# Transformer block with shared keys on one core: last burst cut 384 and 128, w2 kept as tile pairs, wo split on GpSimd, new attention orders

## The chip, the cores and the metric

The kernel runs on one core of a Trainium2 chip: TensorE (PE) multiplies, VectorE (DVE), ScalarE (ACT) and GpSimd (POOL) work on elements, and SyncE (SP) issues most DMAs. Each engine takes its own instructions strictly in the order in which they were written and waits at semaphores for the others. The metric is the device time of one launch in microseconds (us). Three runs of the kernel before took 893.58 to 894.96 us, with a median of 894.08 us.

## What is computed

With x of 2048 rows and 448 columns, 16 heads of 28, one key and one value head that all heads share, and an MLP of 1792 columns:

```python
def _A_ref(x, wq, wk, wv, wo):
    q = (x @ wq).reshape(B, S, H, Dh).transpose(0, 2, 1, 3)
    k = x @ wk
    v = x @ wv
    scores = jnp.einsum("bhqd,bkd->bhqk", q, k) * (Dh ** -0.5)
    p = _softmax(scores, axis=-1)
    o = jnp.einsum("bhqk,bkd->bhqd", p, v)
    return o.transpose(0, 2, 1, 3).reshape(B, S, H * Dh) @ wo

def _B_ref(x, w1, b1, w2, b2):
    y = _layernorm(x, axis=-1)
    h = _gelu(jnp.einsum("bsd,df->bsf", y, w1) + b1)
    return jnp.einsum("bsf,fd->bsd", h, w2) + b2

xn = _layernorm(x, axis=-1)
return x + _A_ref(xn, ...) + _B_ref(xn, ...)
```

All is float32. Where a product is made of float32r operands, each operand is split into a high and a low part and three products are summed (high by high, high by low, low by high).

## The kernel before

The 2048 rows are 16 row tiles of 128, in four chunks of four (512 rows). The program has three stages: norms and the projections of q, k and v (to about 71 us); the MLP, chunk by chunk (to about 349 us); attention with the output projection (to the end).

**MLP.** Slot `n` of the loop at L635 runs `mlp1` for one of the 14 column tiles of the hidden layer (11 matmuls, then three ACT and three DVE operations and a subtraction on POOL that make the high part `hh` and the low part `hl`), and `mlp2` for the tile two slots earlier (12 matmuls: four row tiles by three terms). w2 is not ready when the stage begins: `w2_split(s)` cuts the raw rows of two column tiles, 2s and 2s+1, into a high part on ACT (L381) and a low part on DVE (L382), and issues the load of a later pair. In the first chunk (c = 0) it is called at ft = 0, 3, 5, 7, 9, 11 and 13 (L654), always behind `mlp1` of the same slot. The high parts of all 14 tiles are one tile `w2h`, the low parts one tile `w2l`.

**Attention.** A unit is 512 queries by four heads; there are 16 units, four for each chunk, and each has 16 key tiles of 128. For each key tile `scores` makes 12 matmuls (four heads side by side in the rows of the array, three terms), one PSUM bank for each head, and then ACT takes the exponentials of the four banks (L625) into a tile `p`. The 2nd argument of `scores`, the number behind an `s` in the order, says by its bits which neighbouring banks are taken by one ACT instruction: `s6` makes one of one bank and one of three (1+3), `s5` 2+2, `s2` 1+2+1, `s4` 1+1+2, `s1` 2+1+1, `s0` four of one. Banks that are not neighbours, since the ring of eight wraps round, are never joined. `pv`, a `P` with a number of key tiles behind it, multiplies the exponentials by the values (`vs`, in which a column of ones gives the sums) into one PSUM bank, and DVE adds that bank to `oc` (L733; L731 for the first of a unit).

The PSUM banks are a ring of eight: every `s` takes the next four, every `P`, `m` and `Q` the next one. Who takes a bank must wait until the one that had it eight takes earlier has been read out, by ACT for an `s` bank and by DVE for the others.

What sets the order is the table `ORDERS` (L34 to L36): one line for units 0 to 3, one for units 4 to 14, one for the last. Two key tiles are scored ahead while the MLP ends, so the `s` of a line are two key tiles ahead of its `P`. Beside `s` and `P` there are `m` (find the shift for the exponentials of the next unit: one matmul, four DVE operations, a small DMA), `Q` (output projection of one row tile of the chunk before: 12 matmuls), `T` (the part of it that can be done early for the last chunk: 9 matmuls) and `E3` (the last burst). `load_unit(u + 1)` is issued on SP when unit u starts, and `m` reads what it loads.

When the last `P` of a unit is done, `norm_jobs` puts three DVE operations behind the next `P` and three more, and a POOL subtraction, behind the third `P`.

`split_out` cuts wo into a high and a low part (two passes over 1792 columns on DVE). It is called behind the third word of unit 0. The first use of its result is the first `Q`, in unit 4.

**Last burst.** `last_burst` multiplies the last three key tiles of unit 15 in two halves of 256 queries. Each half goes through a chain of five DVE operations, and the second one also through six small ones of `flag`; then two matmuls for each half (L776) finish the four row tiles, which are added to the rest on DVE (row tile 1: ACT copies, POOL adds) and stored, by SP for row tiles 0 and 2 and by ACT's queue for 1 and 3.

Of the kernel before, what the change touches and what calls it, by code (L numbers as in the profile page):

```python
# [10 lines left out]
F32 = mybir.dt.float32  # L11
F32R = mybir.dt.float32r
# [18 lines left out]
MLP_ORDER = 1, 2, 3, 0  # L31
HD = D // 2
WEIGHTS = 7
ORDERS = ("s5 P1 s6 s6 P2 s6 s5 P2 s4 s1 m P2 s6 P1 s6 s5 P2 s6 s6 P2 s6 s5 P2 s6 s4 P2",  # L34
          "s5 P1 s6 s6 P2 s6 s5 P2 s6 s6 P2 s6 s5 P2 s2 s2 P2 s2 m Q s2 s6 P3 s6 s4 P2",
          "s5 P1 s6 s6 P2 s6 s5 P2 s6 s6 P2 s6 s5 P2 s2 s2 P2 s2 m Q s2 s6 P2 T T T E3")  # L36
FIRST_BANK = 0
LIMITS = 0.25, 2.0 ** 40

# [2 lines left out]
def block_kernel(ctx, tc, x, wq, wk, wv, wo, w1, b1, w2, b2, out):  # L42
# [4 lines left out]
    def f(t):  # L47
        return t.bitcast(F32)
# [327 lines left out]

    def w2_split(s):
        raw = wl_q.pop(0)
        ab = slice(2 * s, 2 * s + 2)

        act.activation(w2h[:, ab, :], raw, AF.Copy, scale=0.5)  # L381
        dve.scalar_tensor_tensor(w2l[:, ab, :], raw, 0.5, f(w2h[:, ab, :]), op0=ALU.mult, op1=ALU.subtract)  # L382
        if s + 2 < NF // 2:
            w2_load(s + 2)

# [189 lines left out]
    def mlp2(c, ft, then=None):  # L575
        if ft == 0:
            m2s[c] = [bank(CT + k, (P, D)) for k in range(CT)]
        m2 = m2s[c]
        hh, hl = hs.pop((c, ft))
        terms = ((hh, w2h), (hh, w2l), (hl, w2h))  # L580
        parted = c == 0 and ft == 0
        if parted:
            for k in range(CT):
                for i, (h, w) in enumerate(terms[:2]):
                    pe.matmul(m2[k], h[:, k * P:(k + 1) * P], w[:, ft, :], start=(i == 0), stop=False)
        for k in range(CT):
            for i, (h, w) in enumerate(terms):
                if parted and i < 2:
                    continue
                pe.matmul(m2[k], h[:, k * P:(k + 1) * P], w[:, ft, :], start=(ft == 0 and i == 0),  # L590
                          stop=(ft == NF - 1 and i == 2))
# [87 lines left out]
    woh, wol = weights_tile(), weights_tile()  # L679

    def split_out():
        dve.tensor_copy(woh, wor)
        dve.tensor_sub(wol, wor, f(woh))


    sums = keep.tile([P, NU, CW // 32], F32, name="sums")
# [62 lines left out]
    def last_burst(n, flag):  # L749
        u = NU - 1  # L750
        c, g = units[u]
        oc = pos.pop(u)
        tr, rb = (att.tile([P, CW], F32, name=name) for name in ("tr2", "tr"))
        rc = att.tile([P, CW // 32], F32, name="rc")
        halves = [(slice(256 * i, 256 * i + 256), slice(8 * i, 8 * i + 8)) for i in range(2)]
        sides = []
        for h, r in halves:
            po = score_bank()[:, 0:256]
            for k in range(NT - n, NT):
                for j in range(4):  # L760
                    pe.matmul(po[32 * j:32 * j + 32, :], vs[:, k, :], ps[u, k][:, j, h],
                              start=(k == NT - n), stop=(k == NT - 1))
            sides.append(po)
        ahead(CT - 1)
        for i, (h, r) in enumerate(halves):
            dve.tensor_add(oc[:, h], oc[:, h], sides[i])
# [4 lines left out]
            dve.transpose(blocks(rb[:, h]), rc[:, r, None].to_broadcast([P, 8, 32]))  # L771
            dve.tensor_mul(oc[:, h], oc[:, h], rb[:, h])
            if i == 1:
                copy()
            for k in (2 * i, 2 * i + 1):
                pe.matmul(outs[k], oc[:, k * P:(k + 1) * P], wor[:, g, :], start=False, stop=True)  # L776
        for k in range(CT):
            a = rows[c, k]
            if k == 1:
                act.activation(tr[:, 0:D], outs[k], AF.Copy)  # L780
                pool.tensor_add(a, a, tr[:, 0:D])
            else:
                dve.tensor_add(a, a, outs[k])
            (nc.scalar if k % 2 else nc.sync).dma_start(ov[:, CT * c + k, :], a)
# [117 lines left out]
```

## Time and profile before

| | us |
|---|---|
| median of three runs | 894.08 |
| the profiled execution, its own time | 893.52 |
| its span on the core | 891.7 |
| TensorE busy in the span | 875.2 (98%) |
| ScalarE busy | 650.1 (73%) |
| VectorE busy | 360.7 (40%) |
| GpSimd busy | 155.3 (17%) |

The mean granted clock of TensorE is 0.997. Times in the rows are counted from the start of the span; 1.8 us of the profiled execution lie outside it. In a timeline row stand the start, the length, engine and line, what is written and read, the shape, how many instructions were merged, and in brackets how long the engine sat idle before and what ended that. A float32 matmul of `pv` shows as two instructions, so a `P2` counts x16 and an `s` x12. Matmuls overlap, so the time that a burst holds TensorE is read from its start to the start of the next one, not from its length. Now and then a matmul's record is missing.

### The profile page before, as it was taken

Reading aid. Unit: us, or ns where it says so; the run is one execution under the profiler, and the core shown is the slowest. Engines: PE = TensorE matmul, PEld = TensorE weight load, DVE = VectorE, ACT = ScalarE, POOL = GpSimd, SP = SyncE. Lnnn points to the kernel's source line nnn. Section 1 sums busy time; section 2 is a strip of 40 time slices with the busy share of each in tenths; the row PEclk is TensorE's granted clock in tenths of the full one; section 3 lists DMA queues with packets and bytes.
Section 4 is the critical chain, followed back from the end, with each engine's and each line's share of the span. In section 5 each row is a group of like instructions: output and inputs, shape, how many; then the busy total and the mean of one; then the engine's idle time right before and its main releaser. Section 6 shows DMA issues by size and latency. Waiting matters only on the chain.

```text
span 891.7 us, 16976 instructions
## 1 busy us (share of the span) xinstructions
PE 875.2 (98%) x6997; PEld 529.5 (59%) x6997; DVE 360.7 (40%) x654; ACT 650.1 (73%) x890; POOL 155.3 (17%) x149
## 2 busy tenths in 40 slices
PE   9999999999999999899999999999999999999997
PEld 8877888888888886333434444444444444444444
DVE  7865454335345353342343234233233233333323
ACT  5765443333443436799999898898898899899891
POOL 7443243242234332000000000000000000000000
PEclk9999999999999999999999999999999999999999
DMA  9792112002001103000002101102101102102001
GB/s 301 215 288 81 42 63 83 1 1 83 21 21 51 44 11 91 9 22 22 9 16 64 33 1 33 33 2 74 32 1 33 33 1 74 33 1 73 12 1 54
DMA packets 28957, 46.02 MB, mean 52 GB/s; under 512 B 4542, under 2 KB 20492, under 8 KB 28876
## 3 DMA queue, kind: packets, MB, share of 16 engines
q1 hardware_dynamic: 27468, 44.32, 16.1%
q8 instruction: 56, 0.92, 0.4%
q10 hardware_dynamic: 1408, 0.57, 0.2%
q14 instruction: 25, 0.20, 0.1%
HBM read 28.22 MB, written 14.68 MB: 48 GB/s over the span
## 4 chain that ended last, share of the span: by engine, by line
PE 87%; ACT 7%; issue 2%; DVE 2%; DMA 1%; SPq 0%; DVEq 0%; ACTq 0%
PE banks L618 24%; PE banks L739 23%; PE banks L180 15%; PE banks L590 15%; ACT p L625 5%; PE banks L701 4%; PE banks L185 2%; PE banks L183 2%; PE banks L304 1%; PE banks L523 1%; DMA xl<-in_A_wo_dram 1%; DMA qd<-qe 0%; DVE w2l L382 0%; PE banks L776 0%; DMA rows<-in_A_x_dram 0%
## 5 line engine op out<-in xcount | busy, mean ns | idle before, releaser
L625 ACT ACTIVATE p<-banks 128x1024 f32<-128x1024 f32 (+2 forms) x623 | 484.8, 879 | 39.5 <-PE banks L618 36.4
L618 PE MATMUL banks<-xh,ks 32*128 32x512 f32 x3072 | 256.1, 424 | 6.4 <-DVE oc L733 4.3
L618 PEld LDWEIGHTS banks<-xh,ks 32*128 32x128 f32 x3072 | 145.0, 183 | 168.0 <-ACT p L625 142.7
L739 PE MATMUL banks<-p,vs 128*32 128x512 f32 x2008 | 243.4, 601 | 0.0
L733 DVE TENSOR_TENSOR oc<-oc,banks 128x512 f32<-128x512 f32 x115 | 78.9, 686 | 304.0 <-PE banks L739 245.9
L739 PEld LDWEIGHTS banks<-p,vs 128*32 128x32 f32 x2008 | 52.2, 109 | 120.9 <-issue 80.4
L564 ACT ACTIVATE hx<-banks,b1t 128x512 f32<-128x512 f32 x56 | 38.5, 688 | 110.7 <-PE banks L185 103.7
L572 POOL TENSOR_TENSOR hl<-hx,hh 128x512 fp32r<-128x512 f32 x56 | 76.8, 1371 | 182.3 <-DVE hh L571 176.9
L723 POOL TENSOR_TENSOR otl<-oc,oth 128x512 fp32r<-128x512 f32 x15 | 19.2, 1280 | 487.7 <-DVE oth L722 487.7
L566 DVE SCALAR_TENSOR_TENSOR hz<-hz,hx 128x512 f32<-128x512 f32 x56 | 44.3, 792 | 101.6 <-ACT hz L565 101.3
L590 PE MATMUL banks<-w2l,hh 128*128 128x448 f32 x220 | 81.0, 368 | 0.8 <-DVE w2l L382 0.7
L590 PE MATMUL banks<-w2h,hl 128*128 128x448 f32 x224 | 81.4, 366 | 0.0
L590 PE MATMUL banks<-w2h,hh 128*128 128x448 f32 x220 | 81.0, 368 | 0.1
L567 ACT ACTIVATE hz<-hz 128x512 f32<-128x512 f32 x56 | 35.4, 632 | 48.5 <-DVE hz L566 48.5
L180 PE MATMUL banks<-xl,w1h 128*128 128x512 f32 x168 | 65.7, 391 | 0.0
L180 PE MATMUL banks<-xh,w1l 128*128 128x512 f32 x168 | 65.6, 391 | 0.0
L180 PE MATMUL banks<-xh,w1h 128*128 128x512 f32 x168 | 65.5, 390 | 0.0
L568 DVE SCALAR_TENSOR_TENSOR hx<-hz,hx 128x512 f32<-128x512 f32 x56 | 39.1, 698 | 42.9 <-ACT hz L567 42.9
L590 PEld LDWEIGHTS banks<-w2l,hh 128*128 128x128 f32 x220 | 41.3, 188 | 7.1 <-DVE w2l L382 3.2
L590 PEld LDWEIGHTS banks<-w2h,hh 128*128 128x128 f32 x220 | 41.3, 188 | 6.0 <-issue 0.7
L590 PEld LDWEIGHTS banks<-w2h,hl 128*128 128x128 f32 x224 | 42.1, 188 | 3.3
L565 ACT ACTIVATE hz<-banks,b1s 128x512 f32<-128x512 f32 x56 | 38.2, 682 | 0.0
(156 smaller groups left out, 765.3 us busy)
## 6 DMA issues: line engine op xcount, KB each, us to landing
xh<-qd SPq DMA_DIRECT2D x64, 112.0 KB
qd<-qe SPq DMA_DIRECT2D x12, 512.0 KB
a<-in_A_x_dram SPq DMA_DIRECT2D x24, 224.0 KB
ad<-a SPq DMA_DIRECT2D x16, 224.0 KB
row<-ad SPq DMA_DIRECT2D x16, 224.0 KB
raw<-in_B_w_dram SPq DMA_DIRECT2D x7, 448.0 KB
out_dram<-row SPq DMA_DIRECT2D x14, 224.0 KB
ks<-qe SPq DMA_DIRECT2D x16, 112.0 KB
```

The source lines that it names most:

```text
L180: pe.matmul(ps, w, v, start=(n == 0), stop=False)
L564: act.activation(hx, ph, AF.Identity, bias=b1t[:, ft:ft + 1])
L565: act.activation(hz, ph, AF.Square, bias=b1s[:, ft:ft + 1], scale=GELU[0] ** 0.5)
L566: dve.scalar_tensor_tensor(hz, hz, 1.0, hx, op0=ALU.add, op1=ALU.mult)
L568: dve.scalar_tensor_tensor(hx, hz, 1.0, hx, op0=ALU.add, op1=ALU.mult)
L572: pool.tensor_sub(hl, hx, f(hh))
L590: pe.matmul(m2[k], h[:, k * P:(k + 1) * P], w[:, ft, :], start=(ft == 0 and i == 0), stop=(ft == NF - 1 and i == 2))
L618: pe.matmul(bank(at[j]), ks[rs, i, keys], qss[u][rs, h, :], start=(n == 0), stop=(n == 2))
L625: act.activation(p[:, j:j + n, :], banks[:, at[j]:at[j] + n, :], AF.Exp, scale=SCALE)
L701: pe.matmul(po, ots[c, g][o][:, ts], w[:, g, :], start=(n == 1), stop=(stop and n == 3 * len(gs)))
L733: dve.tensor_add(pos[u], pos[u], po)
L739: pe.matmul(po[32 * j:32 * j + 32, :], vs[:, k, :], ps[u, k][:, j, :], start=(k == kt), stop=(k == kt + n - 1))
```

## The change

Five things are changed.

1. `ORDERS` is new. Units 0 to 3 now have `P1` behind every `s`. Units 4 to 14 have `s P1` eight times, then `s6 P2 s4 s4 m Q s0 s1 P3 s6 s4 P2 s2 P1`; the last unit begins in the same way and ends in `s6 T T T E3`. The ACT instructions of the exponentials go from 629 (332 of one bank, 199 of two, 98 of three) to 802 (598, 186 and 18).
2. `split_out` runs on POOL and is called behind the third word of unit 2.
3. w2's parts are 14 tiles, a high and a low one for each pair, and `w2_split` is called in the even slots 0, 2, ..., 12.
4. The last burst is cut into 384 and 128 queries, so three row tiles hang on the first part and one on the second.
5. At the end row tiles 0 and 1 go through ACT and POOL (in before row tile 1 only), with a tile `half` of their own, and 2 and 3 through DVE.

```diff
-ORDERS = ("s5 P1 s6 s6 P2 s6 s5 P2 s4 s1 m P2 s6 P1 s6 s5 P2 s6 s6 P2 s6 s5 P2 s6 s4 P2",
-          "s5 P1 s6 s6 P2 s6 s5 P2 s6 s6 P2 s6 s5 P2 s2 s2 P2 s2 m Q s2 s6 P3 s6 s4 P2",
...
+ORDERS = ("s2 P1 s4 P1 s2 P1 s2 P1 s1 P1 m s2 P1 s4 P1 s2 P1 s2 P1 s2 P1 s4 P1 s4 P1 s4 P1 s2 P1 s2 P1 s2 P1",
+          "s2 P1 s2 P1 s2 P1 s2 P1 s2 P1 s4 P1 s4 P1 s0 P1 s6 P2 s4 s4 m Q s0 s1 P3 s6 s4 P2 s2 P1",
...
     def w2_split(s):
         raw = wl_q.pop(0)
-        ab = slice(2 * s, 2 * s + 2)
-
-        act.activation(w2h[:, ab, :], raw, AF.Copy, scale=0.5)
-        dve.scalar_tensor_tensor(w2l[:, ab, :], raw, 0.5, f(w2h[:, ab, :]), op0=ALU.mult, op1=ALU.subtract)
+        high, low = w2s[s]
+        act.activation(high, raw, AF.Copy, scale=0.5)
+        dve.scalar_tensor_tensor(low, raw, 0.5, f(high), op0=ALU.mult, op1=ALU.subtract)
...
-    w2h = hp.tile([P, NF, D], F32R, name="w2h", bufs=1)
-    w2l = hp.tile([P, NF, D], F32R, name="w2l", bufs=1)
+    w2s = [[hp.tile([P, 2, D], F32R, name=f"w2{n}{s}", bufs=1) for n in "hl"] for s in range(NF // 2)]
...
-        if c == 0 and (ft == 0 or ft % 2 and ft > 1):
+        if c == 0 and ft % 2 == 0:
             w2_split(ft // 2)
...
     def split_out():
-        dve.tensor_copy(woh, wor)
-        dve.tensor_sub(wol, wor, f(woh))
+        pool.tensor_scalar(woh, wor, 1.0, 0.0, op0=ALU.mult, op1=ALU.add)
+        pool.tensor_sub(wol, wor, f(woh))
...
-        halves = [(slice(256 * i, 256 * i + 256), slice(8 * i, 8 * i + 8)) for i in range(2)]
+        cut = 3 * P
+        sides_at = [(slice(0, cut), slice(0, cut // 32)), (slice(cut, CW), slice(cut // 32, CW // 32))]
...
-            for k in (2 * i, 2 * i + 1):
+            for k in range(h.start // P, h.stop // P):
                 pe.matmul(outs[k], oc[:, k * P:(k + 1) * P], wor[:, g, :], start=False, stop=True)
         for k in range(CT):
             a = rows[c, k]
-            if k == 1:
-                act.activation(tr[:, 0:D], outs[k], AF.Copy)
-                pool.tensor_add(a, a, tr[:, 0:D])
+            if k < 2:
+                half = att.tile([P, D], F32, name="half")
+                act.activation(half, outs[k], AF.Copy)
+                pool.tensor_add(a, a, half)
             else:
                 dve.tensor_add(a, a, outs[k])
             (nc.scalar if k % 2 else nc.sync).dma_start(ov[:, CT * c + k, :], a)
...
-            if (u, n) == (0, 2):
+            if (u, n) == (2, 2):
                 split_out()
```

Three places show what that does to the order of the instructions. Lines of the changed kernel are one or two lower than before (L738 is `pv`, L617 `scores`).

On TensorE, in a unit of the second kind, from the `s` that opens the unit; `p_...` is the tile of exponentials of one key tile, and `x24` are two `s` one behind the other. Before:

```order
L618 MATMUL banks<-xh,ks 128x512 x12
L739 MATMUL banks<-p_5751,vs 32x512 x4
L618 MATMUL banks<-xh,ks 128x512 x24
L739 MATMUL banks<-p_5766,vs 32x512 x4
L739 MATMUL banks<-p_5803,vs 32x512 x4
L618 MATMUL banks<-xh,ks 128x512 x24
L739 MATMUL banks<-p_5829,vs 32x512 x4
L739 MATMUL banks<-p_5845,vs 32x512 x4
```

After the change, from the same place:

```order
L617 MATMUL banks<-xh,ks 128x512 x12
L738 MATMUL banks<-p_5874,vs 32x512 x4
L617 MATMUL banks<-xh,ks 128x512 x12
L738 MATMUL banks<-p_5890,vs 32x512 x4
L617 MATMUL banks<-xh,ks 128x512 x12
L738 MATMUL banks<-p_5915,vs 32x512 x4
L617 MATMUL banks<-xh,ks 128x512 x12
L738 MATMUL banks<-p_5948,vs 32x512 x4
```

Two scores and two products in a row have become one and one; the matmuls themselves are the same.

On VectorE, at the start of unit 0, before; L595 closes the MLP, `xl` stands for the tiles of wo here, L731 and L733 read the `P` banks, L524 to L530 are `m`:

```order
L595 TENSOR_TENSOR a<-a,banks 128x448 x4
L731 COPY oc<-banks 128x512
L682 CAST xl<-xl 128x1792
L683 TENSOR_TENSOR xl<-xl 128x1792
L733 TENSOR_TENSOR oc<-oc,banks 128x512 x2
L524 STREAM_TRANSPOSE tm<-banks 128x512
```

and on GpSimd, from the end of the MLP on, after the change (`otl` is the low part that `norm_jobs` makes, one for each unit):

```order
L675 MEMSET xl 128x1792
L686 MEMSET sums 128x256
L722 TENSOR_TENSOR otl<-oc,oth 128x512
L681 TENSOR_SCALAR xl<-xl 128x1792
L682 TENSOR_TENSOR xl<-xl 128x1792
L722 TENSOR_TENSOR otl<-oc,oth 128x512 x14
```

The two passes over wo have left VectorE's queue and stand in GpSimd's, behind the `otl` of unit 0 (made in unit 1) and ahead of that of unit 1.

On VectorE, in the first slots of the MLP, before (three operations for each `mlp1`, then `w2_split`):

```order
L571 CAST hh<-hx 128x512
L382 SCALAR_TENSOR_TENSOR w2l<-raw,w2h 128x896
L566 SCALAR_TENSOR_TENSOR hz<-hz,hx 128x512
L568 SCALAR_TENSOR_TENSOR hx<-hz,hx 128x512
L571 CAST hh<-hx 128x512
L566 SCALAR_TENSOR_TENSOR hz<-hz,hx 128x512
L568 SCALAR_TENSOR_TENSOR hx<-hz,hx 128x512
L571 CAST hh<-hx 128x512
L566 SCALAR_TENSOR_TENSOR hz<-hz,hx 128x512
L568 SCALAR_TENSOR_TENSOR hx<-hz,hx 128x512
L571 CAST hh<-hx 128x512
L382 SCALAR_TENSOR_TENSOR w2l<-raw,w2h 128x896
```

After the change:

```order
L569 CAST hh<-hx 128x512
L381 SCALAR_TENSOR_TENSOR w2l_856<-raw,w2h_855 128x896
L564 SCALAR_TENSOR_TENSOR hz<-hz,hx 128x512
L566 SCALAR_TENSOR_TENSOR hx<-hz,hx 128x512
L569 CAST hh<-hx 128x512
L564 SCALAR_TENSOR_TENSOR hz<-hz,hx 128x512
L566 SCALAR_TENSOR_TENSOR hx<-hz,hx 128x512
L569 CAST hh<-hx 128x512
L381 SCALAR_TENSOR_TENSOR w2l_858<-raw,w2h_857 128x896
```

The second pair, and each one behind it, is now cut one slot earlier, and into a tile of its own.

More of the change, by code (lines that the diff above doesn't have):

```diff
@@ L33 @@
 WEIGHTS = 7
-ORDERS = ("s5 P1 s6 s6 P2 s6 s5 P2 s4 s1 m P2 s6 P1 s6 s5 P2 s6 s6 P2 s6 s5 P2 s6 s4 P2",
-          "s5 P1 s6 s6 P2 s6 s5 P2 s6 s6 P2 s6 s5 P2 s2 s2 P2 s2 m Q s2 s6 P3 s6 s4 P2",
-          "s5 P1 s6 s6 P2 s6 s5 P2 s6 s6 P2 s6 s5 P2 s2 s2 P2 s2 m Q s2 s6 P2 T T T E3")
+ORDERS = ("s2 P1 s4 P1 s2 P1 s2 P1 s1 P1 m s2 P1 s4 P1 s2 P1 s2 P1 s2 P1 s4 P1 s4 P1 s4 P1 s2 P1 s2 P1 s2 P1",
+          "s2 P1 s2 P1 s2 P1 s2 P1 s2 P1 s4 P1 s4 P1 s0 P1 s6 P2 s4 s4 m Q s0 s1 P3 s6 s4 P2 s2 P1",
+          "s2 P1 s2 P1 s2 P1 s2 P1 s2 P1 s4 P1 s4 P1 s0 P1 s6 P2 s4 s4 m Q s0 s1 P3 s6 T T T E3")
 FIRST_BANK = 0
@@ L579, in mlp2 @@
         hh, hl = hs.pop((c, ft))
-        terms = ((hh, w2h), (hh, w2l), (hl, w2h))
+        high, low = (w[:, ft % 2, :] for w in w2s[ft // 2])
+        terms = ((hh, high), (hh, low), (hl, high))
         parted = c == 0 and ft == 0
@@ L584, in mlp2 @@
                 for i, (h, w) in enumerate(terms[:2]):
-                    pe.matmul(m2[k], h[:, k * P:(k + 1) * P], w[:, ft, :], start=(i == 0), stop=False)
+                    pe.matmul(m2[k], h[:, k * P:(k + 1) * P], w, start=(i == 0), stop=False)
         for k in range(CT):
@@ L589, in mlp2 @@
                     continue
-                pe.matmul(m2[k], h[:, k * P:(k + 1) * P], w[:, ft, :], start=(ft == 0 and i == 0),
+                pe.matmul(m2[k], h[:, k * P:(k + 1) * P], w, start=(ft == 0 and i == 0),
                           stop=(ft == NF - 1 and i == 2))
@@ L754, in last_burst @@
         rc = att.tile([P, CW // 32], F32, name="rc")
-        halves = [(slice(256 * i, 256 * i + 256), slice(8 * i, 8 * i + 8)) for i in range(2)]
+        cut = 3 * P
+        sides_at = [(slice(0, cut), slice(0, cut // 32)), (slice(cut, CW), slice(cut // 32, CW // 32))]
         sides = []
-        for h, r in halves:
-            po = score_bank()[:, 0:256]
+        for h, r in sides_at:
+            po = score_bank()[:, 0:h.stop - h.start]
             for k in range(NT - n, NT):
@@ L764, in last_burst @@
         ahead(CT - 1)
-        for i, (h, r) in enumerate(halves):
+        for i, (h, r) in enumerate(sides_at):
             dve.tensor_add(oc[:, h], oc[:, h], sides[i])
@@ L770, in last_burst @@
             dve.reciprocal(rc[:, r], blocks(tr[:, h])[:, :, 0])
-            dve.transpose(blocks(rb[:, h]), rc[:, r, None].to_broadcast([P, 8, 32]))
+            dve.transpose(blocks(rb[:, h]), rc[:, r, None].to_broadcast([P, r.stop - r.start, 32]))
             dve.tensor_mul(oc[:, h], oc[:, h], rb[:, h])
```

## The prediction

> **What bounds the kernel now.** First the page: the busy times and the chain that ended last.
>
> ```profile
> PE 875.2 (98%) x6997; PEld 529.5 (59%) x6997; DVE 360.7 (40%) x654; ACT 650.1 (73%) x890; POOL 155.3 (17%) x149
> PE 87%; ACT 7%; issue 2%; DVE 2%; DMA 1%; SPq 0%; DVEq 0%; ACTq 0%
> ```
>
> TensorE is the end's path nearly throughout, so an edit is worth what it takes from TensorE's time line. The busy share doesn't show what can be taken, since overlapping matmuls hide short waits; I therefore read the starts of bursts in TensorE's timeline. Four `s` that open units 0, 1, 4 and 15:
>
> ```profile
> 348.91 0.97 PE L618 MATMUL banks<-xh,ks 32*128 32x512 f32 x12
> 386.24 0.97 PE L618 MATMUL banks<-xh,ks 32*128 32x512 f32 x12
> 479.59 0.97 PE L618 MATMUL banks<-xh,ks 32*128 32x512 f32 x12
> 843.33 0.97 PE L618 MATMUL banks<-xh,ks 32*128 32x512 f32 x12
> ```
>
> Unit 0 takes 37.33 us, units 1 to 3 93.35/3 = 31.12 each, units 4 to 14 363.74/11 = 33.07 each. Unit 0 has the work of units 1 to 3 and is 6.2 longer. Inside unit 4 and into 5:
>
> ```profile
> 501.65 0.50 PE L523 MATMUL banks<-xh,kd 128*128 128x512 f32 x1
> 504.51 1.74 PE L618 MATMUL banks<-xh,ks 32*128 32x512 f32 x24
> 506.22 2.78 PE L739 MATMUL banks<-p,vs 128*32 128x512 f32 x24
> 508.93 1.92 PE L618 MATMUL banks<-xh,ks 32*128 32x512 f32 x24
> 510.78 1.92 PE L739 MATMUL banks<-p,vs 128*32 128x512 f32 x16
> 512.64 0.97 PE L618 MATMUL banks<-xh,ks 32*128 32x512 f32 x12
> 513.54 1.06 PE L739 MATMUL banks<-p,vs 128*32 128x512 f32 x8
> 514.54 2.21 PE L618 MATMUL banks<-xh,ks 32*128 32x512 f32 x24
> 516.67 1.92 PE L739 MATMUL banks<-p,vs 128*32 128x512 f32 x16
> ```
>
> From start to start: `m Q` 2.86; a pair of `s` 1.71 behind `Q`, 1.85 behind `P3`, 2.13 behind `P1`; `P3` 2.71, `P2` 1.86, `P1` 1.00; a single `s` 0.90. So `P` costs 0.855 a key tile and 0.145 a burst, always; a pair of `s` costs anything from 1.71 to 2.13. The pairs hold the waits: the second `s` needs the banks of the last `s` of the pair before, whose exponentials aren't done.
>
> How fast can ScalarE give banks back? Its instructions behind `Q` (the first row is two of them merged, then each of the next three by itself):
>
> ```profile
> 505.57 1.51 ACT L625 ACTIVATE p<-banks 128x512 f32<-128x512 f32 x2 [1.75 <-PE banks L618]
> 506.06 1.02 ACT L625 ACTIVATE p<-banks 128x1024 f32<-128x1024 f32 x1
> 506.97 0.60 ACT L625 ACTIVATE p<-banks 128x512 f32<-128x512 f32 x1
> 507.45 0.62 ACT L625 ACTIVATE p<-banks 128x512 f32<-128x512 f32 x1
> ```
>
> Two banks are followed after 0.91, one after 0.48: 0.43 a bank and 0.05 an instruction. Their lengths overlap.
>
> **Term 1, the orders: split `s` and `P` one by one.** Without a wait, `s P1` is 0.90 + 1.00 = 1.90 a key tile. The pairs of unit 5 take (2.13 + 1.86)/2 = 2.00 on what this window shows, and nearer 1.9 elsewhere. More bursts cost 0.145 for each `P` and some 0.05 for each group of `s`; the waits inside the pairs go. So the question is whether waits come back. Going through the ring for `s P1 s P1`: bank 4 of an `s` is the one that bank 1 of the `s` before had, and `P` takes its bank 2. Exponentials start when an `s` is done, which I put 1.07 behind its start (504.51 to 505.57, where ScalarE sat idle). Bank 1 is then free at 1.07 + 0.60 = 1.67, and the next `s` comes at 1.90. With 1+2+1, banks 2 and 3 are free at 1.07 + 0.48 + 1.02 = 2.57, and `P` comes at 1.90 + 0.90 = 2.80. Both have some 0.2 to spare. ScalarE needs 4 x 0.43 + 3 x 0.05 = 1.87 a key tile (1.92 with four single banks), beside TensorE's 1.90: no backlog grows. `P1` beside `P2` gives DVE more adds, 12 instead of 8 a unit at 0.69; `norm_jobs` holds DVE for some 2.5 us behind the third `P`, which makes the next add 0.6 late, and the bank is needed 1.9 behind the end of its `P`. It is hidden.
>
> Units 1 to 3: 16 x 1.90 + 0.43 for `m` = 30.75 (with 1.895), beside 31.12: -0.37 each, **-1.1**. Units 4 to 14: nine `s P1` 17.06, `s6 P2` 2.75, `s4 s4` 1.85 (behind a `P2`, so DVE's add of that bank is waited for as behind `P3`), `m Q` 2.86, `s0 s1` 1.71, `P3` 2.71, `s6 s4` 1.85, `P2` 1.86: 32.65, beside 33.07. ScalarE sits idle around `Q` (1.75 in the row at 505.57), so a backlog from the pairs there is gone before the next unit. -0.42 by eleven: **-4.6**. Unit 15 has other words behind `Q`. Up to `m` a unit of before takes 33.07 - (512.64 - 501.65) = 22.08, and the new one 8 x 1.895 + 2.75 + 1.85 = 19.76; behind `Q` the new one has `P3 s6` (2.71 + 0.90) where the old one had `P2` (1.86), and the rest is the same: **-0.6**. Bounds: all the waits come back (0), or one finds `s4 s4` free of them too (-8).
>
> [...] Here the spacing decides.
>
> **Term 2, unit 0.** Where its 6.2 us are lost:
>
> ```profile
> 349.96 1.74 SPq L678 DMA_DIRECT2D xl<-in_A_wo_dram  x4
> 351.74 3.33 SPq L538 DMA_DIRECT2D xh<-qd  x4
> 354.74 1.49 PE L618 MATMUL banks<-xh,ks 32*128 32x512 f32 x15
> 356.64 1.09 DVE L682 CAST xl<-xl 128x1792 fp32r<-128x1792 f32 x1 [4.94 <-DMA xl<-in_A_wo_dram]
> 359.81 0.68 DVE L733 TENSOR_TENSOR oc<-oc,banks 128x512 f32<-128x512 f32 x1
> 360.54 1.48 PE L618 MATMUL banks<-xh,ks 32*128 32x512 f32 x9 [4.31 <-DVE oc L733]
> ```
>
> DVE waits for wo, splits it, and only then adds up a `P` bank that TensorE needs: the second `s` stands still until 360.54. On POOL nobody waits for the split before unit 4. Taking it away gives back 37.33 - 31.12 = 6.2. What is late next is `m`: it now comes behind five `s P1`, at 348.91 + 5 x 1.90 = 358.4, and reads what the four loads at 351.74 bring. The wo loads ended issue at 351.70 and let DVE go at 356.64, 4.9 later; by the same delay the loads of unit 1, issued to 355.07, are there at about 360 at the latest. I take 359.5, so 1.1 us of wait (0 to 1.6). Unit 0 becomes 30.75 + 1.1 = 31.85: **-5.5**.
>
> What POOL does instead isn't free for certain. Two rows from the MLP, and from the page POOL's subtraction when alone:
>
> ```profile
> 132.90 1.09 DVE L382 SCALAR_TENSOR_TENSOR w2l<-raw,w2h 128x896 fp32r<-128x896 f32 x1
> 133.15 1.98 POOL L572 TENSOR_TENSOR hl<-hx,hh 128x512 fp32r<-128x512 f32 x1 [2.71 <-PE banks L185]
> L723 POOL TENSOR_TENSOR otl<-oc,oth 128x512 fp32r<-128x512 f32 x15 | 19.2, 1280 | 487.7 <-DVE oth L722 487.7
> ```
>
> Beside a DVE operation the POOL one takes 1.98 instead of 1.28, about as much longer as DVE had left to run (0.84): one blocks the other. The subtraction over 1792 columns is 1.28 x 3.5 = 4.5 at most. It starts in unit 1, behind the `otl` of unit 0, near `m` of that unit; if a DVE operation is held for all of it, an add comes 4.5 late, with about 1.9 to spare: 0 to +3, once. I take **+0.4**, near the lower end, since DVE's adds read one operand from PSUM and few DVE operations there are like the one above.
>
> [...]
>
> **Term 3, w2.**
>
> ```profile
> 97.64 2.43 PE banks L590 x12
> 102.58 2.69 PE banks L590 x12
> 132.94 0.36 PE L590 MATMUL banks<-w2h,hh 128*128 128x448 f32 x1
> 134.04 0.47 PE L590 MATMUL banks<-w2l,hh 128*128 128x448 f32 x1 [0.74 <-DVE w2l L382]
> ```
>
> `mlp2` is 2.43, but in the even slots it waits for a pair that was cut one slot before: 2.69 at 102.58, and in the last such slot 1.10 between two matmuls that are 0.2 apart elsewhere. Five slots at about 0.26 and one at 0.9 are 2.2. Cut a whole slot (4.9 us) earlier, the pair is there in time, and with tiles of its own the odd slot doesn't read what is being written. ACT's 0.94 and DVE's 1.09 are the same work as before, the raw loads come along one slot earlier on SP, which has nothing else near. **-2.2** (0 to -2.5); `mlp2` of the first tile still waits for the first pair.
>
> **Term 4, the end.**
>
> ```profile
> 877.60 2.80 PE L761 MATMUL banks<-p,vs 128*32 128x256 f32 x48
> 879.22 0.42 DVE L766 TENSOR_TENSOR oc<-oc,banks 128x256 f32<-128x256 f32 x1 [6.46 <-PE banks L761]
> 882.25 1.67 PE L776 MATMUL banks<-xl,oc 128*128 128x448 f32 x4
> 883.53 0.42 DVE L772 TENSOR_TENSOR oc<-oc,tr 128x256 f32<-128x256 f32 x1
> 884.57 1.13 POOL L781 TENSOR_TENSOR row<-row,tr 128x448 f32<-128x448 f32 x1 [30.98 <-ACT tr L780]
> 885.74 1.09 ACTq L784 DMA_DIRECT2D out_dram<-row  x2
> ```
>
> Counted from 877.60: the first half is ready at 1.62, the second chain ends at 6.35, the last two matmuls at about 8.0, the last DMA is issued at 8.9. With 384 queries the first part is ready 0.6 later, its five operations are 0.13 longer each where they run over all columns (0.68 for 512 at 359.81, 0.42 for 256), so three matmul pairs of some 0.8 (two in 1.67) start at 4.9 and the fourth ends at about 8.0 again. The first is through ACT's copy (an exponential of that size takes 0.60) at about 6.5. But POOL now adds two rows one behind the other, 6.5 + 2 x 1.13 = 8.8, and row 1's DMA stands ahead of row 3's in ACT's queue: last issue at 9.2. **+0.3** (-0.5 to +1).
>
> **Sum.** -1.1 - 4.6 - 0.6 - 5.5 + 0.4 - 2.2 + 0.3 = -13.3 from the profiled 893.52: 880.2. The median of the runs is 0.56 higher, so 880.8 for a median.
>
> **Rivals.**
> - *The orders give nothing*: `s P1` runs at ScalarE's pace with its waits, 1.95 a key tile, where the gain of a late unit (0.42 over eight or nine) is used up. For: only 0.02 lies between 1.92 and 1.90, and chains of `s P1` don't occur in before. Against: each lone `s P1` shows 0.90 + 1.00. Then terms 2 to 4 are left: 887.
> - *The stall moves*: POOL's pass holds DVE, or `m` waits longer in unit 0, 3 to 5 us of term 2 come back: 885.
> - *ScalarE becomes the bound, slower*: an instruction costs by its length, not by its spacing.
>
> ```profile
> L625 ACT ACTIVATE p<-banks 128x1024 f32<-128x1024 f32 x197 | 195.5, 1041 | 5.1 <-PE banks L618 5.1
> L625 ACT ACTIVATE p<-banks 128x512 f32<-128x512 f32 x328 | 186.3, 608 | 34.4 <-PE banks L618 31.4
> ```
>
>  Two single banks are 1.216 beside 1.041 for a joined one: 0.175 an instruction, by 173 that is 30 us. It decides from the point where 27.5 (64 banks) and 50 instructions pass 33.07, at 0.11 each; at 0.175 a late unit is 36.2, and the kernel some 50 us slower: 944. Against: by lengths a unit of before (20 single, 13 double and 6 triple ones, a triple at 1.04 + 0.43) would already be 34.5, longer than its 33.07.
> - *It doesn't do what it says*: the waits on w2 and wo stay with other names, and the orders balance: 894.
>
> **How the numbers follow.** Forecast 0.70, orders nothing 0.14, stall moves 0.08, ScalarE bound 0.04, nothing at all 0.04. The range takes the forecast's own bounds (a few us either way), the first two rivals, and ends at 888.5; below, no `m` wait and freer pairs give 876. A measurement of this kernel can tell about 0.2% from no change, 1.8 us: faster 0.92, same 0.04, slower 0.04.
>
> **What would show it.** In the changed profile: unit 0 as long as units 1 to 3 but for one wait of about 1 us at `m`; `s P1` at 1.90 from start to start, with ScalarE's instructions 0.48 and 0.91 apart; late units of 32.6; every `mlp2` but the first at 2.43; POOL's two passes over wo early in unit 1 with no DVE row stretched to 4 us beside them; last DMA issue about 9.2 behind the start of the last burst. Wrong would be a wait in `P1` for exponentials in every key tile, or one of about 3 us in unit 1.

## The result, and the profile after

| | before | after |
|---|---|---|
| median (five runs each), us | 894.12 | 887.44 |
| lowest to highest, us | 893.58 to 894.96 | 887.22 to 890.4 |
| the profiled execution, its own time, us | 893.52 | 887.44 |
| its span, us | 891.7 | 885.6 |

The ratio of after to before is 0.9931, with a 95% interval of 0.9916 to 0.9947: faster, by half of what was forecast. First the busy times and the chain of waits on the page of after:

```profile
PE 872.1 (98%) x6997; PEld 514.7 (58%) x6997; DVE 412.3 (47%) x726; ACT 654.5 (74%) x1064; POOL 162.6 (18%) x152
PE 94%; DVE 2%; DMA 1%; ACT 1%; issue 1%; SPq 1%; POOL 0%; DVEq 0%; ACTq 0%; POOLq 0%
```

ScalarE, 7% of the chain before, has shrunk to 1%: nearly all the waits for exponentials are gone. These shares don't tell what came in their place. As before, the starts of bursts do. TensorE's timeline of after (start, length, engine, line, operation), at the openings of units 0, 1, 2, 4 and 15 and of the last burst:

```profile
346.68 0.97 PE L617 MATMUL banks<-xh,ks 32*128 32x512 f32 x12
...
378.56 0.97 PE L617 MATMUL banks<-xh,ks 32*128 32x512 f32 x12
...
414.33 0.97 PE L617 MATMUL banks<-xh,ks 32*128 32x512 f32 x12
...
475.88 0.97 PE L617 MATMUL banks<-xh,ks 32*128 32x512 f32 x12
...
837.35 0.97 PE L617 MATMUL banks<-xh,ks 32*128 32x512 f32 x12
...
870.75 1.18 PE L761 MATMUL banks<-p,vs 128*32 128x384 f32 x12
```

From these starts and those of before (unit 2 opens there at 417.28) follows where the span's 6.1 us come from:

| stretch | before | after | difference | forecast |
|---|---|---|---|---|
| up to unit 0 | 348.91 | 346.68 | -2.2 | -2.2 |
| unit 0 | 37.33 | 31.88 | -5.5 | -5.5 |
| **unit 1** | 31.04 | **35.77** | **+4.7** | 0.0 (-0.37 + 0.4) |
| units 2 and 3 | 62.32 | 61.55 | -0.8 | -0.7 |
| units 4 to 14 | 363.74 | 361.47 | -2.3 | -4.6 |
| unit 15 | 34.27 | 33.40 | -0.9 | -0.6 |
| last burst to the end | 14.12 | 14.88 | +0.8 | +0.3 |

Most of the shortfall lies in unit 1. The chain that ended last, step by step (start, length, what), jumps over to other engines there, and it also holds the forecast wait of `m` in unit 0 (a DMA, until 357.20):

```profile
352.06 5.14 DMA xh<-qd
390.42 3.98 DVE mn L528
396.83 1.87 PE banks L738 x8
```

`mn` is the third DVE operation of `m`: 16 elements in each partition. The timelines of GpSimd, VectorE and TensorE at that place in after:

```profile
388.56 1.70 POOL L681 TENSOR_SCALAR xl<-xl 128x1792 fp32r<-128x1792 f32 x1
390.34 4.00 POOL L682 TENSOR_TENSOR xl<-xl 128x1792 fp32r<-128x1792 f32 x1
```

```profile
389.69 0.69 DVE L524 TENSOR_REDUCE mr<-tm 128x16 f32<-128x512 f32 x1
390.42 3.96 DVE L528 TENSOR_SCALAR mn<-mr 128x16 fp32r<-128x16 f32 x1
394.41 0.71 DVE L529 STREAM_TRANSPOSE tm<-mn 128x512 f32<-128x512 f32 x1
395.05 1.47 DVE L732 TENSOR_TENSOR oc<-oc,banks 128x512 f32<-128x512 f32 x2
```

```profile
392.37 0.49 PE L617 MATMUL banks<-xh,ks 32*128 32x512 f32 x2
395.75 1.07 PE L617 MATMUL banks<-xh,ks 32*128 32x512 f32 x10 [2.89 <-DVE oc L732]
396.76 1.94 PE L738 MATMUL banks<-p,vs 128*32 128x512 f32 x8
398.62 1.53 PE L617 MATMUL banks<-xh,ks 32*128 32x512 f32 x12
400.08 1.07 PE L738 MATMUL banks<-p,vs 128*32 128x512 f32 x8
```

Read them from the top. GpSimd subtracts over wo from 390.34 to 394.34. `mn` starts at 390.42 and ends at 394.38, 0.04 after the subtraction. The add of a `P` bank, next on VectorE but one, comes at 395.05, and the third matmul of an `s`, which takes that bank, stands until 395.75. That `s` takes 4.39 from start to start instead of 0.90 (3.49 lost); the `P` behind it takes 1.86 instead of 1.00 and the next `s` 1.46 instead of 0.90: 1.42 more. ScalarE isn't behind there; it sits idle for 3.07 until 396.60. What has changed is TensorE's granted clock. The windows view of after has it as the last number but two:

```profile
396.50:399.80 3.30, 3.30 (x22) 1.04 (x20) 0.71 (x2) 2.00 (x3) 0.00 (x0) 0.50 0.00 1
```

At half the clock a matmul of that `P` takes 1.06 instead of 0.59; from 394 to 396 and from 400 on the clock is 1.00. Before has the same behind its stop of 4.31 in unit 0: 0.50 from 361.0 to 364.1. So the 4.9 us are 3.49 around the stop and 1.42 at the slower clock behind it, all from an instruction that is otherwise 0.17 long.

### The profile page after: what moved, and what is told of

The parts are those of the page before. It is cut to its first block, busy times and chain, and to the rows that moved or that the text cites. A ratio compares the mean times of both kernels' runs of the same rounds, so it can differ in the third digit from the quotient of the medians.

```text
span 885.6 us, 17300 instructions
## 1 busy us (share of the span) xinstructions
PE 872.1 (98%) x6997; PEld 514.7 (58%) x6997; DVE 412.3 (47%) x726; ACT 654.5 (74%) x1064; POOL 162.6 (18%) x152
## 4 chain that ended last, share of the span: by engine, by line
PE 94%; DVE 2%; DMA 1%; ACT 1%; issue 1%; SPq 1%; POOL 0%; DVEq 0%; ACTq 0%; POOLq 0%
PE banks L738 27%; PE banks L617 25%; PE banks L180 16%; PE banks L589 15%; PE banks L700 4%; PE banks L185 2%; PE banks L183 2%; PE banks L304 1%; PE banks L432 1%; PE banks L522 1%; DMA xh<-qd 1%; DMA qd<-qe 1%; DVE mn L528 0%; ACT p L624 0%; SPq L537 0%
## 5 line engine op out<-in xcount | busy, mean ns | idle before, releaser
L624 ACT ACTIVATE p<-banks 128x512 f32<-128x512 f32 (+2 forms) x796 | 488.8, 783 | 31.8 <-PE banks L617 31.6
L738 PE MATMUL banks<-p,vs 128*32 128x512 f32 x2008 | 258.6, 604 | 0.0
L617 PE MATMUL banks<-xh,ks 32*128 32x512 f32 x3072 | 247.1, 422 | 3.0 <-DVE oc L732 2.9
L617 PEld LDWEIGHTS banks<-xh,ks 32*128 32x128 f32 x3072 | 135.9, 184 | 193.9 <-issue 93.9
L732 DVE TENSOR_TENSOR oc<-oc,banks 128x512 f32<-128x512 f32 x190 | 130.4, 686 | 244.5 <-PE banks L738 230.3
L738 PEld LDWEIGHTS banks<-p,vs 128*32 128x32 f32 x2008 | 44.9, 108 | 102.1 <-ACT p L624 53.8
```

The source lines that it names most:

```text
L617: pe.matmul(bank(at[j]), ks[rs, i, keys], qss[u][rs, h, :], start=(n == 0), stop=(n == 2))
L624: act.activation(p[:, j:j + n, :], banks[:, at[j]:at[j] + n, :], AF.Exp, scale=SCALE)
L732: dve.tensor_add(pos[u], pos[u], po)
```

## The experiments

The times of the kernels below are medians of their runs; a ratio is to the kernel before, timed beside them. Theory A, as the expectations call it, says that GpSimd's subtraction holds `mn` for as long as it runs (3.96 instead of 0.17 in after) and that this is all of unit 1's loss: without it unit 1 falls to 30.8. Against it stand a price of the pass itself, wherever it runs, and one of the new early order.

**1. The pass elsewhere on GpSimd.** In after, `split_out` is called in unit 4, ahead of `Q` and away from any `m`. By theory A unit 1 then takes 30.8, unit 4 still 32.8, and the kernel about 882.5:

```diff
-            if (u, n) == (2, 2):
+            if (u, n) == (4, 6):
```

> The changed kernel with split_out called behind the seventh word of unit 4 instead of the third of unit 2, still on GpSimd, so that its two passes stand behind the otl of unit 3 and run in unit 4 ahead of m. [...] Rival B (GpSimd's passes slow TensorE or VectorE wherever they run): unit 4 becomes some 4 to 5 us longer and the time stays at 887. Rival C (unit 1 is long for another reason, its loads or its m): unit 1 stays at 35.8, 887.

Measured: 882.7 us, ratio 0.9871 (0.9854 to 0.9887). Unit 1 takes 30.85 and unit 4, where the pass now runs, 32.81 like its neighbours; all 16 `mn` take 0.174 to 0.176. The pass itself costs nothing; 4.7 us are back.

**2. The same place, in pieces.** Four pieces of 448 columns, copy and subtraction in turns, still in unit 1:

```diff
-        pool.tensor_scalar(woh, wor, 1.0, 0.0, op0=ALU.mult, op1=ALU.add)
-        pool.tensor_sub(wol, wor, f(woh))
+        for g in range(NG):
+            pool.tensor_scalar(woh[:, g, :], wor[:, g, :], 1.0, 0.0, op0=ALU.mult, op1=ALU.add)
+            pool.tensor_sub(wol[:, g, :], wor[:, g, :], f(woh[:, g, :]))
```

> The changed kernel with each of split_out's two passes over 1792 columns cut into four of 448, alternating, at the same place (they run in unit 1). Theory A (a lock for a whole instruction): L528 waits for one piece at most, about 1.1 us instead of 3.96, which is inside what the next bank can spare; unit 1 near 31 to 31.5, time about 883. Rival B (GpSimd's work slows VectorE by its amount, not by the length of one instruction): the eight pieces take some 6 us as well and unit 1 stays near 35; 887.

Measured: 882.8 us, 0.9869 (0.9852 to 0.9885), unit 1 at 30.83. The timelines of GpSimd and of VectorE in this run:

```profile
389.19 1.15 POOL L683 TENSOR_TENSOR xl<-xl 128x448 fp32r<-128x448 f32 x1
390.31 0.57 POOL L682 TENSOR_SCALAR xl<-xl 128x448 fp32r<-128x448 f32 x1
```

```profile
390.39 0.51 DVE L528 TENSOR_SCALAR mn<-mr 128x16 fp32r<-128x16 f32 x1
```

`mn` is held again, until the piece ends that is running (390.88), and no longer: it slips in ahead of the next one. Same work, same place; it is the length of the blocking instruction that counts. Here it is a copy of 0.57; had `mn` met a subtraction, it would have been 1.15 at most, an estimate from the length of the piece in the first row. The 0.34 lost are hidden.

**3. The pass back on VectorE**, in the place that after gives it in the program (behind the third word of unit 2):

```diff
-        pool.tensor_scalar(woh, wor, 1.0, 0.0, op0=ALU.mult, op1=ALU.add)
-        pool.tensor_sub(wol, wor, f(woh))
+        dve.tensor_copy(woh, wor)
+        dve.tensor_sub(wol, wor, f(woh))
```

> The changed kernel with split_out back on VectorE (copy 1.09, subtraction 2.02 us), called behind the third word of unit 2. Nothing waits for wo's load there. Theory A: unit 1 falls to 30.8; in unit 2 the next add of a P bank comes about 3.1 us late, with 1.9 to spare, so unit 2 becomes 1 to 2.5 us longer than 30.7; about 884. Rival (VectorE has the room, the engine was never the trouble, only the wait for the load): unit 2 stays at 30.7, 882.5. Rival C (unit 1 is long for another reason): 888.

Measured: 883.99 us, 0.9878 (0.9861 to 0.9894). Unit 1 is free (30.83), unit 2 takes 32.51 instead of 30.72. VectorE's and TensorE's timelines:

```profile
413.27 1.03 DVE L681 CAST xl<-xl 128x1792 fp32r<-128x1792 f32 x1
414.34 2.02 DVE L682 TENSOR_TENSOR xl<-xl 128x1792 fp32r<-128x1792 f32 x1
```

```profile
417.01 0.96 PE L617 MATMUL banks<-xh,ks 32*128 32x512 f32 x10 [1.30 <-DVE oc L732]
417.91 1.06 PE L738 MATMUL banks<-p,vs 128*32 128x512 f32 x8
418.90 0.97 PE L617 MATMUL banks<-xh,ks 32*128 32x512 f32 x12
419.80 1.06 PE L738 MATMUL banks<-p,vs 128*32 128x512 f32 x8
```

3.1 us of VectorE in one piece make TensorE stand for 1.30, and the `P1` and the `s` behind that take 0.99 and 0.90 from start to start, their usual times. So the change's pass on GpSimd cost more in after (4.9) than it would have cost on VectorE there (1.8).

**4. `m` moved out from under the pass.** After as it is, the pass in unit 1 and all, but `m` of the early order behind the eighth `s P1` instead of the fifth:

```diff
-ORDERS = ("s2 P1 s4 P1 s2 P1 s2 P1 s1 P1 m s2 P1 s4 P1 s2 P1 s2 P1 s2 P1 s4 P1 s4 P1 s4 P1 s2 P1 s2 P1 s2 P1",
+ORDERS = ("s2 P1 s4 P1 s2 P1 s2 P1 s2 P1 s2 P1 s4 P1 s1 P1 m s2 P1 s2 P1 s4 P1 s4 P1 s4 P1 s2 P1 s2 P1 s2 P1",
```

> The changed kernel with split_out as changed (GpSimd, behind the third word of unit 2, running in unit 1), and in the order of units 0 to 3 m moved three steps back, behind the eighth s P1 instead of the fifth, with the s1 that stands ahead of it. Theory A (the loss in unit 1 is the meeting of m's L528 with GpSimd's subtraction; the wait in unit 0 is m ahead of its loads): L528 now starts some 5.7 us later, after the subtraction has ended, so unit 1 falls from 35.8 to 30.8 without touching the split, and unit 0 from 31.9 to 30.8: 6 us less than the changed kernel, 881.4. Rival (GpSimd's passes cost TensorE time wherever m stands): unit 1 stays near 35; 886.

Measured: 881.68 us, 0.9859 (0.9842 to 0.9875); units 0 to 3 take 30.72, 30.85, 30.72 and 30.72. GpSimd and VectorE in unit 1:

```profile
388.97 4.05 POOL L682 TENSOR_TENSOR xl<-xl 128x1792 fp32r<-128x1792 f32 x1
```

```profile
390.77 0.69 DVE L732 TENSOR_TENSOR oc<-oc,banks 128x512 f32<-128x512 f32 x1 [1.21 <-PE banks L738]
392.67 0.69 DVE L732 TENSOR_TENSOR oc<-oc,banks 128x512 f32<-128x512 f32 x1 [1.21 <-PE banks L738]
...
394.74 0.17 DVE L528 TENSOR_SCALAR mn<-mr 128x16 fp32r<-128x16 f32 x1
```

The two adds inside GpSimd's 4.05 us take their usual 0.69; one of their operands comes from PSUM. In after `mn` alone was held, and here, behind the pass, it takes 0.17. Not every operation within SBUF is held: in after `L524`, from `tm` to `mr`, took its usual 0.69 beside GpSimd's first pass (its row starts at 389.69, the pass lasts until 390.26). The wait of `m` in unit 0 for its load is gone as well: 30.72 instead of the 31.54 of experiment 1.

**5. The w2 edit alone**, put into the kernel before (tiles of pairs and even slots; the slots are this line, the tiles are those of the change):

```diff
-        if c == 0 and (ft == 0 or ft % 2 and ft > 1):
+        if c == 0 and ft % 2 == 0:
```

> The kernel before with the w2 edit alone (14 tiles, split in the even slots). Theory: 2.2 us of waits in the even slots go, nothing else moves: 891.9 against 894.1, each mlp2 but the first at 2.43, attention as before. Rival (what is won in the MLP is lost at its end or in unit 0, whose stall hangs on the load of wo): 893.5 to 894.

Measured: 892.02 us, 0.9971 (0.9962 to 0.9981): 2.6 less than the 894.62 of before beside it. The chain of waits has the `mlp2` of its first chunk one behind the other:

```profile
79.86 2.43 PE banks L589 x12
84.80 2.43 PE banks L589 x12
```

In that chunk all from here on take 2.43, where before every second one took 2.69 or more. In the profiled execution (893.3) the first `mlp2` stood longer, with a granted clock of 0.83 around it; that run is 1.3 above the median. The windows view has the clock ahead of the DMA share, as the last number but two:

```profile
70.00:80.00 10.00, 8.33 (x31) 6.66 (x30) 5.99 (x9) 5.41 (x9) 4.28 (x3) 0.83 0.15 47
```

**6. Which half of it?** Before with the even slots only, w2's parts still one tile each:

> The kernel before with one part of the w2 edit alone: splits in even slots only, w2h and w2l still one tile each over all 28 key tiles. If waits come by tile (a reader of one slice waits for the last write to the whole tile), the even mlp2 of the first pass that read behind a later split wait: some of the first 14 stay at 2.6 or more above the 2.43 of e4. If waits come by slice, the first pass is as in e4, every mlp2 but the first in 2.43, and the time is e4's, 892.0, to within 0.5: then the slots gave the 2.2 us and the pairs nothing.

Measured: 892.38 us in its one run, and the chain:

```profile
77.50 2.43 PE banks L590 x12
82.44 2.43 PE banks L590 x12
```

With one tile for all parts, no `mlp2` behind the first waits for a later split, and unit 0 opens at 346.70, as in after (346.68). So the slots do all of the 2.2 us before unit 0, and the tiles of pairs give nothing that this run shows. (Its unit 0 took 1.1 longer than that of before, 38.47, which hides part of the gain in the total: behind its stop of 4.28 the `P2` took 3.57 from start to start, where that of before took 2.93.)

**7. The old orders.** Experiment 1 with the three lines of `ORDERS` as before:

> e1_split_unit4 with the three old orders, everything else as changed. Theory (the new orders are worth what the units show): units 1 to 3 at 31.1 instead of 30.8, units 4 to 14 at 33.05 instead of 32.85, the last 34.3 instead of 33.4, and unit 0, where m now comes later, 31.1 instead of 31.5: 0.9 + 2.3 + 0.9 - 0.4, 3.7 us more, 886.4. Rival (without the stalls of wo the orders bring nothing): 882.7.

Measured: 885.79 us, 0.9903 (0.9886 to 0.9919), 3.1 slower than experiment 1. By the starts of TensorE's rows the old orders cost 1.0 in units 1 to 3, 2.1 in units 4 to 14 and 0.9 in unit 15, and save 0.4 in unit 0, where `m` has no wait. So the new orders give 3.6 us in the profile, not the 6.3 of the forecast.

**8. Why `Q` is dearer.** Experiment 1 with three more bursts ahead of the late order's `m Q`:

```diff
-          "s2 P1 s2 P1 s2 P1 s2 P1 s2 P1 s4 P1 s4 P1 s0 P1 s6 P2 s4 s4 m Q s0 s1 P3 s6 s4 P2 s2 P1",
+          "s2 P1 s2 P1 s2 P1 s2 P1 s2 P1 s4 P1 s4 P1 s0 P1 s2 P1 s4 P1 s4 m Q s0 s1 P3 s6 s4 P2 s2 P1",
```

> e1 (the splitting pass in unit 4) with the late order's m Q placed behind three more bursts of one tile: s0 P1 s2 P1 s4 P1 s4 m Q instead of s0 P1 s6 P2 s4 s4 m Q. Theory: Q's 3.02 instead of the 2.86 of before is a wait for ScalarE, which frees the bank that Q takes late, because 14 score groups stand in a row ahead of Q there. Then m Q is back at 2.86 and units 4 to 14 lose 0.16 less, while one P burst more costs 0.1: unit 32.7 instead of 32.77, median 882.0 to 882.5 (e1 had 882.7). Rival: m Q at 3.02 is the price of the place behind short bursts; then m Q stays at 3.02 and the unit is 32.9, median 883.9 or more.

Measured: 884.59 us, 0.9885 (0.9869 to 0.99), 1.9 slower than experiment 1: the theory as put there fails. But one unit of this run differs from the other ten. TensorE and its weight loads in units 7 and 8 (`m`, the first loads of `Q`, the `s` behind `Q`):

```profile
590.28 0.49 PE L522 MATMUL banks<-xh,kd 128*128 128x512 f32 x1
590.78 0.30 PEld L700 LDWEIGHTS banks<-xl,oth 128*128 128x128 f32 x2 [0.31 <-ACT p L624]
...
593.42 0.74 PE L617 MATMUL banks<-xh,ks 32*128 32x512 f32 x8
...
623.28 0.50 PE L522 MATMUL banks<-xh,kd 128*128 128x512 f32 x1
623.38 0.42 PEld L700 LDWEIGHTS banks<-xl,oth 128*128 128x128 f32 x2
...
626.13 0.73 PE L617 MATMUL banks<-xh,ks 32*128 32x512 f32 x8
```

In unit 7 `Q` waits for an exponential, and `m Q` takes 593.42 - 590.28 = 3.14. In unit 8 it doesn't wait and takes 2.85, and the unit 32.72, as the theory put it. So it is a wait for ScalarE, but not one that three bursts ahead take away: `Q` takes a bank of the `s` before last, and only with a `P2` between the last two `s`, as the kernel before has it, was it always free. The rival's "price of the place" is this wait. Why it was free in unit 8 was not found.

**9 and 10. The end.** VectorE's last multiplication took 1.20 us in after beside GpSimd's two row additions. From its timeline at the end:

```profile
877.36 2.27 POOL L782 TENSOR_TENSOR row<-row,half 128x448 f32<-128x448 f32 x2 [30.18 <-ACT half L781]
877.42 1.20 DVE L772 TENSOR_TENSOR oc<-oc,tr 128x128 f32<-128x128 f32 x1
...
878.68 1.02 PE L776 MATMUL banks<-xl,oc 128*128 128x448 f32 x2 [0.36 <-DVE oc L772]
...
879.65 1.10 ACTq L785 DMA_DIRECT2D out_dram<-row  x2
```

Both operands of `L772` are in SBUF. It ends 0.15 behind the first of the two additions (878.48), and the last two matmuls wait for it. Two ways out, both on top of experiment 1. One row tile by GpSimd instead of two, cut as in after (384 and 128):

```diff
-            if k < 2:
+            if k == 1:
```

> e1_split_unit4 (split_out in unit 4, 882.7 us) with the last burst still cut 384 and 128, but only row tile 1 through ScalarE and GpSimd as in the kernel before, row tile 0 through VectorE. In the changed kernel the second part's multiplication on VectorE (L772, 128 columns, two operands in SBUF) took 1.20 us instead of about 0.29 beside GpSimd's first row addition, and the last two matmuls and the last row wait for it. Theory: GpSimd starts only when row 1 is copied, after that multiplication; it takes 0.3 again, and the stretch from the start of the last burst to the end falls from 14.9 to about 14.2 us (882.0). Rival (the 384 part itself makes the end later, since its chain is longer): L772 short again, but the stretch stays at 14.9.

Two row tiles by GpSimd, cut in halves (256 and 256):

```diff
-        cut = 3 * P
+        cut = 2 * P
```

> e1_split_unit4 with the last burst cut into 256 and 256 again, row tiles 0 and 1 through ScalarE and GpSimd. Theory (the lock makes the end late): row tile 0 is ready earlier than with 384, GpSimd's first addition begins about when the second half's multiplication (256 columns) does, so whether that is held decides: 14.1 to 14.9 us from the start of the burst to the end, with L772's length telling which. Rival (the cut of 384 costs): 14.1 whatever L772 shows.

Measured: 882.83 us (0.9872, 0.9856 to 0.9888), no gain, and 881.61 us (0.9855, 0.9838 to 0.9871). With one row tile `L772` takes 0.29, but VectorE's row additions (`L784`) begin late:

```profile
872.13 0.29 DVE L772 TENSOR_TENSOR oc<-oc,tr 128x128 f32<-128x128 f32 x1
...
873.20 1.66 DVE L784 TENSOR_TENSOR row<-row,banks 128x448 f32<-128x448 f32 x3
...
873.83 0.86 SPq L785 DMA_DIRECT2D out_dram<-row  x2
873.98 1.28 ACTq L785 DMA_DIRECT2D out_dram<-row  x2
```

The last burst starts at 865.45 here, so the row additions begin 7.75 behind it (before: 6.55) and the last issue ends 9.81 behind it. The lock is gone, yet the stretch from the last burst to the end is 15.30: the theory fails, and what was put down as the rival, that the cut of 384 itself makes the end late, fits. In halves the stretch is 14.35. With the two runs of experiments 11 and 12 below all four combinations are measured; this is when the last issue ends, counted from the start of the last burst:

| | one row tile by GpSimd | two |
|---|---|---|
| 256 and 256 | 9.23 (before), 9.21 (experiment 12) | 9.36 (experiment 10), 9.35 (experiment 11) |
| 384 and 128 | 9.81 (experiment 9) | 10.00 (after) |

The cut costs about 0.6 with either number of row tiles, the second row tile with its lock 0.1 to 0.2. What follows behind the last issue says less: with the end of after unchanged, the profiles of experiments 1 to 4, 7 and 8 have 4.9 to 5.3 there, so the 5.5 of experiment 9 is hardly outside that.

**11 and 12. Both repairs together.** After with `m` as in experiment 4 and the halves of experiment 10; and the same with one row tile by GpSimd:

> The changed kernel with m behind the eighth s P1 of the early order (as in e8) and the last burst cut 256 and 256 (as in e6), row tiles 0 and 1 by ScalarE and GpSimd. If the two gains are independent (the lock in unit 1 and the lock on L772 at the end are two separate waits): unit 1 at 30.8, the last DMA issue at about 8.95 after the burst's start, tail 14.4 instead of e8's 15.0, median 881.0 to 881.2 (e8 had 881.68). If the tail's gain of e6 was chance: 881.7, tail 14.9.

> e10 with only row tile 1 by ScalarE and GpSimd, as the kernel before had it: rows 0, 2 and 3 by VectorE. If what costs at the end is the lock by GpSimd's row additions and the spacing of the DMAs: one GpSimd addition less but one VectorE addition more of 0.5 us, last issue at 8.9 to 9.3 after the burst's start, tail 14.1 (the kernel before) to 14.7; median within 0.3 of e10. If the second row by GpSimd is a gain by itself, e10 is the faster by 0.4 or more.

Measured: 880.98 us, 0.9847 (0.9834 to 0.9861), and 881.0 us, 0.9848 (0.9834 to 0.9861). Either beats both kernels: 13.6 below before, 6.5 below after. From the timeline of the first:

```profile
864.86 2.15 PE L761 MATMUL banks<-p,vs 128*32 128x256 f32 x36
...
870.76 0.42 DVE L772 TENSOR_TENSOR oc<-oc,tr 128x256 f32<-128x256 f32 x1
...
871.08 2.23 POOL L782 TENSOR_TENSOR row<-row,half 128x448 f32<-128x448 f32 x2 [29.82 <-ACT half L781]
...
873.34 0.87 ACTq L785 DMA_DIRECT2D out_dram<-row  x2
```

The multiplication starts before GpSimd's first addition and isn't held. The last issue ends 9.35 behind the burst's start and the end comes 14.32 behind it, in the second kernel 14.55: who adds the second row tile makes no difference that the times show.

## Why the prediction was right and wrong

The forecast was 880.8, in a range of 876.0 to 888.5; 887.44 lies in the range, and the direction was right. The size was not: 6.7 us faster instead of 13.3. That the range holds it is in part luck, since its upper end leans on the 887 of a rival that did not come true.

- **The step that failed** is the second half of term 2, "I take +0.4, near the lower end". It was +4.9. That one engine holds the other had been read correctly from the two rows of the MLP (1.98 beside a VectorE operation, 1.28 alone), and both the place (near `m` of unit 1) and the length (4.5 at most, 4.0 measured) were right. Wrong was the reason for the choice, that "few DVE operations there are like the one above". One such operation is enough, and `m` brings it: `mn` reads and writes SBUF alone. The prediction doesn't name it; it asked about the adds. What counted is how long the blocker had left to run: 3.92 in after, where `mn` took 3.96, and 0.49 in experiment 2, where it took 0.51. Experiments 1 and 4 take that meeting away and experiment 2 shortens it, and each brings unit 1 back to 30.8. The prediction's own sign of being wrong, a wait of about 3 us in unit 1, is the 2.89 of the profile.
- The upper bound, "+3, once", was too low too: it counted 4.5 less 1.9 to spare. `mn` was held 3.79 too long and 3.49 of that reached TensorE, so about 0.3 was to spare there, not 1.9. And the 1.42 at a granted clock of 0.50 behind the stop was not in the sum at all.
- This was the rival "the stall moves: POOL's pass holds DVE", at 0.08. Its chance was too small, though its mechanism stood ready with two rows for it. The time, 887, was that of another rival, "the orders give nothing", and experiment 7 excludes that one: agreement with a time alone doesn't pick the mechanism.
- No run shows the 0.4 itself. Its other reason, that an add with one operand in PSUM is not held, was the author's estimate; experiment 4 then showed two such adds beside the pass not held (0.69 each), and what came in place of the 0.4 is the 4.9 of `mn`.
- **Term 1** was right in its mechanism and too large for units 4 to 14: -2.3 instead of -4.6. `s P1` ran at 1.89 to 1.90 a key tile at the head of all units 4 to 14, and units 2 and 3 came out at -0.77 against -0.74. But "`m Q` 2.86" was taken over from before, and it depends on what stands ahead of it. TensorE and its weight loads in unit 5 of after:

```profile
528.48 0.51 PE L522 MATMUL banks<-xh,kd 128*128 128x512 f32 x1
528.85 0.30 PEld L700 LDWEIGHTS banks<-xl,oth 128*128 128x128 f32 x2 [0.18 <-ACT p L624]
...
531.50 1.33 PE L617 MATMUL banks<-xh,ks 32*128 32x512 f32 x16
```

 531.50 - 528.48 = 3.02, 0.16 more, with a wait for ScalarE at `Q`'s first weights that the forecast had ring arithmetic for and didn't apply to `Q`. With it the sum of the parts is 32.81, and nine of the eleven units take 32.77 to 32.84. The other two take 0.4 more (33.20 and 33.13): in unit 8 the pair `s6 s4` takes 2.19 instead of 1.85, in unit 12 `s4 s4` 2.00 and `m Q` 3.14. Why only there stays open.
- That ScalarE could carry 173 more instructions was right: it is busy for 654.5 us instead of 650.1, and the slower rival (944) didn't come. Spacing decided: by the mean lengths in units 4 to 14 of after (0.665 for one bank, 1.092 for two) a 1+2+1 would take 2.42, and `s P1` ran at 1.89 to 1.90.
- **Unit 0** came as worked out: -5.45 for -5.5, and the new wait of `m` for its load cost 1.16 where 1.1 had been put. The 6.2 taken away were not the stop of 4.31 alone, though: most of the rest was the granted clock of 0.50 behind it (for 3.4 us; the `P2` there took 2.93 from start to start instead of 1.86), which the prediction doesn't mention.
- **Term 3** came as worked out, -2.2, and experiment 6 corrects its reason: the slot alone gives it.
- **Term 4** was +0.8 instead of +0.3. The step that failed is that "the fourth ends at about 8.0 again", which puts the cut at nothing: by the table above the cut alone makes the last issue 0.6 later, with the lock and without it. The row additions were counted one behind the other, as measured (2.27), but not what they lock, 0.9 us on `L772`; of that 0.1 to 0.2 is left at the last issue.

## What to carry to other kernels

When a pass moves to GpSimd, list every VectorE instruction that can run beside it and works in SBUF alone, the tiny ones on the critical chain first, and price each at the time that GpSimd's instruction has left, less what the next bank can spare. Here `mn` (3.96 instead of 0.17) and `L772` (1.20 instead of 0.29) were held, the adds that read a bank (0.69) and `L524` (0.69) were not. Then look at the granted clock behind a stop of TensorE: here 2.89 us of standing cost 1.42 more. Where they may meet, cut the pass into pieces or move one of the two; four pieces cost nothing that the times show and held `mn` for 0.51 us in place of 3.96. A duration taken over from the old order (`m Q`) is only good if the banks and buffers it needs come free as early in the new one.

## What had not been expected of the hardware

A VectorE instruction on 16 elements, 0.17 us long, took 3.96 us beside one GpSimd instruction of 4.00. GpSimd's next instruction didn't keep the lock in experiment 2: between two pieces VectorE got in (0.51). And a stop of TensorE cost twice: the granted clock was 0.50 for 3.4 us behind the stop of 2.89 in unit 1 of after and behind that of 4.31 in unit 0 of before; behind the one of 1.30 in experiment 3 a `P1` took its usual 0.99. No experiment was made to find what decides it.
